# Linear attention and Fourier mixing on one core: an own front for the first batch, and a second fold of the channel transform

## The chip, the cores and the metric

The kernel runs on one core of a Trainium2 chip. The metric is the device time of one execution in microseconds. The kernel before takes 449.23 us (median of 3 runs, 448.87 to 451.64). Its profile is of one execution with a span of 447.7 us.

The core's engines are named as in the profile: PE (TensorE, with its weight loads as PEld), DVE (VectorE), ACT (ScalarE), POOL (GpSimd), and SP, whose queue issues stores and DMA transposes. Each engine takes its instructions in the order in which the program lists them.

## What is computed

There are 8 batches, 8 heads, 576 rows, a head size of 64 and 128 features. Per batch, attention with an exponential feature map gives a block of 576 x 512. Its two-dimensional Fourier transform (real part) is added to it, the sum is normalised by row, and two matrices with a ReLU between follow. Cut to the core:

```python
def phi(x):
    proj = einsum('bhsd,df->bhsf', x, w_phi)
    proj = proj - max(abs(proj), axis=-1, keepdims=True)
    return concatenate([exp(proj), exp(-proj)], axis=-1)

q_p, k_p = phi(q), phi(k)
kv = einsum('bhsf,bhsd->bhfd', k_p, v);  z = sum(k_p, axis=2)
x = (q_p @ kv) / (q_p @ z + 1e-6)            # heads side by side: 576 x 512
u = x + real(fft(fft(x, axis=rows), axis=channels))
un = (u - mean(u)) / sqrt(var(u) + 1e-6)     # per row
out = u + relu(un @ w_ch1) @ w_ch2           # 512 -> 2048 -> 512
```

Note that the second half of the features is exp(-proj + max), as the maximum is subtracted before the sign is turned.

## The kernel before

The program is one list of small steps. Each letter of `PLAN` takes the next step of one stream, and the order of the letters is the order of the instructions on every engine. The streams go through the batches one after the other, so steps of three batches stand side by side: `F` forward (68 steps a batch: hidden and output layer), `M` mixing (heads, Fourier transform), `D` row fold, `N` normalise, `T` the exponentials, `P` query maxima, `R` key maxima, `S` scaling of V, `K`, `V`, `Q` loads, `A`, `B` DMA transposes, `W` the large weights, `C` the tables of sines, `G`, `J` the turning of the first batch's K and Q on PE.

```python
PLAN = (
    "GCCGCTGJGCTJKQRJTRTSGTRPTSJTRTTSJMRMWTSSPTMTTBPMPTPVMTTMMMMMPTWATMPMMTMMMTTRRTDDSTMCRMSPTTMMTSTRMTTN"
    ...
```

The tables are made by C steps: DVE makes the angles, ACT takes the sines of them (SS, CS for the rows, SD, CD for the channels) before the first exponentials.

The exponentials of the queries in the feature step, both from one projection `psh`, without the maximum; the maximum of the negative half is put in later as the factor E2 = exp(2 max):

```python
psh = pj.tile([128, 2, 4, 128], F32, tag="pj", name="psh")
...
for sgn, QP in ((1.0, QPHP), (-1.0, QPHN)):
    nc.scalar.activation(out=o, in_=psh[:], func=AT.Exp, scale=sgn)     # L580
```

Numerator and denominator of a head, for all batches:

```python
def combine(h, kvh):
    pn_ = pj.tile([128, 2, 512], F32, tag="pj", name="pn_")
    for c in range(5):
        for i, QP in enumerate((QPHP, QPHN)):
            nc.tensor.matmul(pn_[:, i, 65 * c:65 * c + 65], lhsT=QP[:, h, ...], rhs=kvh[:, i, :],
                             start=True, stop=True)                      # L676
    nc.vector.tensor_tensor(out=tg[:], in0=Bv, in1=E2[...], op=ALU.mult)  # L683
    nc.vector.tensor_tensor(out=cb[:], in0=Av, in1=tg[:], op=ALU.add)     # L688
    nc.vector.reciprocal(out=rd[:], in_=cb[:, :, D:D + 1])                # L690
    nc.gpsimd.tensor_tensor(out=X[:, :, D * h:D * h + D], in0=cb[:, :, 0:D],
                            in1=rd[...], op=ALU.mult)                     # L691
```

The transform uses symmetry. Channels are folded once (FEO holds sums and differences of channel a and its mirror, L623), rows once (CEO and SE, L632 and L637). The first row of each fold is handled apart: it goes to a tile HI, a matmul with ones spreads it to all partitions, and it is subtracted:

```python
nc.scalar.copy(out=HI[0:1], in_=FEO[0:1, 0, :, :])                        # L645
...
pm = pb.tile([128, 2, 256], F32, tag="pb", name="pm")
nc.tensor.matmul(pm[:], lhsT=ones_b[:], rhs=HI[:], start=True, stop=True) # L716
nc.vector.tensor_tensor(out=CEO[0:64, 2], in0=FEO[0:64, 4], in1=pm[0:64], op=ALU.subtract)  # L717
nc.scalar.copy(out=CEO[64:65, 2, :, :], in_=pm[64:65])                    # L720
nc.vector.scalar_tensor_tensor(out=CEO[:, 0:2, 0, :], in0=pm[...], scalar=-2.0, in1=SE[:],
                               op0=ALU.mult, op1=ALU.add)                 # L721
```

The transform along the rows (psD, L737, twice 6 matmuls of 320 columns, and px, L745), then along the channels:

```python
for t in range(3):
    pu = pb.tile([128, C], F32, tag="pb", name="pu")
    for i, (dt_, mat) in enumerate(((DT, CD), (ET, SD))):
        for cc in range(2):
            nc.tensor.matmul(pu[:], lhsT=dt_[:, cc, 128 * t:128 * t + 128], rhs=mat[:, cc, :],
                             start=(i + cc == 0), stop=(i + cc == 2))     # L758
    ...                                                                   # added to X, L763 to L773
```

Normalising: statistics (L786, L787), UN = X - mean (L791 on ACT for the first batch, L795 on DVE for the others), and a DMA transpose to UT in all batches:

```python
nc.sync.dma_start_transpose(out=UT[:, :, 128 * c:128 * c + M], in_=UN[0:M, c, :])   # L799
```

The forward part: 2 halves of 288 rows, 16 x 4 matmuls each, a ReLU on ACT, then five row blocks of the output layer:

```python
for hf in range(2):
    for hh in range(NHH):
        ps = pb.tile([128, 288], F32, tag="pb", name="psf")
        for cc in range(NCC):
            nc.tensor.matmul(ps[:], lhsT=W1b[...], rhs=UT[:, cc, 288 * hf:288 * hf + 288], ...)  # L835
        nc.scalar.activation(out=HT[...], in_=ps[:], func=AT.Relu)        # L840
for c in range(4):
    for hh in range(NHH):
        nc.tensor.matmul(po[:], lhsT=HT[...], rhs=W2b[:, hh, :], ...)     # L847, 512 columns
    ...                                                                   # scaled, added, stored: L853
...                                                                       # last 64 rows: L862, L869
```

Of the kernel before, what the change touches and what calls it, by code (L numbers as in the profile page):

```python
# [17 lines left out]
MAGIC = 12582912.0  # L18


PLAN = (
    "GCCGCTGJGCTJKQRJTRTSGTRPTSJTRTTSJMRMWTSSPTMTTBPMPTPVMTTMMMMMPTWATMPMMTMMMTTRRTDDSTMCRMSPTTMMTSTRMTTN"
    "NRMMMTSMTTNPTMTPPPSMMPTMFFQPNFFMFTFKFFNMMFMFMFFFMFMFFMFMFFAFBFFFVPPTFRFFMFQTRFFFTPFFFFDFTPPRFFDFFTMN"
    "FTSFFSFFMFTFFMKRFSFMPTFFFRTSMMPFNTNNTTTFFFFFNMMSFFMFTTFMTFFTFFAFTFMNFFMNFFMFFMFFMFVPPFFFFMFMFFMFFBPT"
    "FMFFMFMFFMFRFFTPPFFFRFMTFFFFDTPFFRDFFFTFMFFFQTFFRMSTFFKFMMTRSFTFMFMSPFNNFNTTTFMMTFFFFSFFTTFTSFFMTFFF"
    "ATFMFFMNNFFFMNFFMFFVPPMFFMMFFMFFMFMFFFFBMFMFFPTRFFFTMFFFFRMSTFFFDFPPTFRFFDFFKFTFFMTFFFFRMFSFFTMMFTPF"
    "FRMQTSPFFMFSNNTTTNFFMNFMFFMFSFTMFFMTTFFTFFMTNFFMFFMTFNFFAMMFFMFFMFFFMFFFVPPBFFFTPFFMFFMFFMRFTFRFMFFT"
    "DFFFFPPTFFFFRFDFSFTMFKTSFFFMRFFFTMFMTPFFRMMNPFSFNTFNQTTTMMFFFFFMFSFTMFFMTTTFFFFMFTFMFSFFMNTFNFAMNFMF"
    "MFFFMFMFFBMFFPFMFFFVPPTFFFMFFFTRPPFFFRFMTFFDFKFTPFFFRDFSFFFTMFTFFRFSMFFTFMMTFFFRQMPFMTNFTNTSNTTFFFMM"
    "FSSFFFTTTFNFFMTAFFFTFMNFFMFFFMFFMFFNMFVPPFFFMMFMFFMFFMFFBMFFTPFMFFMFFFFRTMRFFTDFFDFFFFFPPTFMRFFFFFMS"  # L30
    "FTFSFSMFMPTFFRMTTNFFRPMNFNFTFFTFSNFFSTFTFFTFMMFTTFFFFTMTNFFMFFMFFMFFMFNFMTFFFMMMFFFMFFMFFMFMFFFFMFMF"
    "FFFFFFDFFFFDFFFFFMFFFFMMFMFFMNFNFFMFFNFFNFFFFFFFFFFFFMFNFFFFFFFFNFFFFFFFFFFFFFFFFFFFFFFFFFFFFFFFFFFF"
    "FFFFFFFFFFFFFFFFFFFFFFFF"
# [4 lines left out]
def kernel(  # L38
# [10 lines left out]
    nc = tc.nc  # L49
# [47 lines left out]
    CD = const.tile([128, 2, C], BF16, name="CD")  # L97
    SD = const.tile([128, 2, C], BF16, name="SD")


    HIS = [const.tile([128, 2, 256], BF16, name=f"HI{i}") for i in range(2)]
    CXS = [const.tile([128, 2, 128], BF16, name=f"CX{i}") for i in range(2)]
# [17 lines left out]
    pn = const.tile([128, 1], F32, name="pn")  # L120
    blk = const.tile([128, 3], F32, name="blk")
    tn = const.tile([128, 2, 128], F32, name="tn")
    ident = const.tile([128, 128], F32, name="ident")
    sg = const.tile([128, 2], BF16, name="sg")
# [7 lines left out]
    def count_all():  # L132
        count(tn[:, 0, :], [[1, 128]], 0, -1)
        for j in range(2):
            count(
                rs[:, 128 * j:128 * j + 128].rearrange("p (a r) -> p a r", r=16),
                [[-32, 8], [2, 16]], 225 + j, 0,
            )
        count(rs[:, 256:NK], [[1, 64]], 256, 0)
        nc.gpsimd.memset(rs[:, 256:257], 0.0)  # L140
        count(pc_i[:, 0:1], [[1, 1]], 0, 1)
        count(pc[:, 0:2], [[1, 2]], 225, 2)
        count(pc[:, 2:3], [[1, 1]], 256, 1)
        nc.gpsimd.memset(pc[0:1, 2:3], 0.0)
        nc.vector.tensor_single_scalar(
            out=ident[:], in_=tn[:, 0, :], scalar=0.0, op=ALU.is_equal
        )
        count(pc[:, 3:4], [[1, 1]], 0, 1)
        count(rc, [[1, C]], 0, 0)
        count(tn[:, 1, :], [[1, 128]], 0, 1)  # L150
        nc.gpsimd.memset(sg[:, 0:1], 1.0)
        nc.gpsimd.memset(sg[:, 1:2], -1.0)

    def constants(b):

        at, t0, t3 = gs[:, 0:3 * NK], gs[:, 1024:1024 + 3 * NK], ga[:, 0:3 * NK]
        scale = 2.0 * np.pi / S * (1.0 - 1e-7)
# [8 lines left out]
        nc.vector.tensor_tensor(  # L166
            out=at.rearrange("p (j n) -> p j n", n=NK),
            in0=rs.unsqueeze(1).to_broadcast([128, 3, NK]),
            in1=pc[:, 0:3].unsqueeze(2).to_broadcast([128, 3, NK]), op=ALU.mult,
        )  # L170
        nc.vector.tensor_scalar(
            out=t0, in0=at, scalar1=1.0 / S, scalar2=MAGIC, op0=ALU.mult, op1=ALU.add
        )
        nc.vector.tensor_scalar(
            out=t0, in0=t0, scalar1=MAGIC, scalar2=-float(S), op0=ALU.subtract, op1=ALU.mult
        )
        nc.vector.tensor_tensor(out=at, in0=at, in1=t0, op=ALU.add)
        nc.scalar.activation(
            out=SS[:].rearrange("p j n -> p (j n)"), in_=at, func=AT.Sin, scale=scale
        )  # L180
        nc.vector.scalar_tensor_tensor(
            out=t3, in0=at, scalar=-1.0, in1=at, op0=ALU.mult, op1=ALU.max
        )
        nc.scalar.activation(
            out=CS[:].rearrange("p j n -> p (j n)"), in_=t3, func=AT.Sin, scale=-scale,
            bias=halfpi[:],
        )
        yield

        t0 = gc[:, C:2 * C]  # L190
        tc2, tc3 = (gc[:, C * i:C * i + C] for i in (2, 3))
        scale_c = 2.0 * np.pi / C * (1.0 - 1e-7)
        nc.vector.tensor_scalar_mul(out=pn[:], in0=pc[:, 3:4], scalar1=1.0 / C)
        nc.vector.tensor_scalar(
            out=t0, in0=rc, scalar1=pn[:], scalar2=MAGIC, op0=ALU.mult, op1=ALU.add
        )
        nc.vector.tensor_scalar(
            out=t0, in0=t0, scalar1=MAGIC, scalar2=-float(C), op0=ALU.subtract, op1=ALU.mult
        )
        nc.vector.scalar_tensor_tensor(  # L200
            out=tc2, in0=rc, scalar=pc[:, 3:4], in1=t0, op0=ALU.mult, op1=ALU.add
        )
        nc.scalar.activation(out=SD[:, 0, :], in_=tc2, func=AT.Sin, scale=-scale_c)
        nc.vector.scalar_tensor_tensor(
            out=tc3, in0=tc2, scalar=-1.0, in1=tc2, op0=ALU.mult, op1=ALU.max
        )
        nc.scalar.activation(
            out=CD[:, 0, :], in_=tc3, func=AT.Sin, scale=-scale_c, bias=halfpi[:]
# [11 lines left out]
        yield  # L220
        for dst in (SS, CS):
            nc.gpsimd.memset(dst[64:65, 2, :], 0.0)
        nc.gpsimd.memset(CS[64:65, 2, 256:257], float(S))
        yield

        turn = sg[:].unsqueeze(1).to_broadcast([128, 128, 2])
        back = sg[:, ::-1].unsqueeze(1).to_broadcast([128, 128, 2])
        for dst, a, src, sign in (
            (CD, 0, CD, turn), (CD, 1, SD, turn), (SD, 0, SD, turn), (SD, 1, CD, back)
        ):  # L230
            nc.gpsimd.tensor_tensor(
                out=dst[:, 1, a::2].rearrange("p (n t) -> p n t", t=2),
                in0=src[:, 0, a::2].rearrange("p (n t) -> p n t", t=2),
                in1=sign, op=ALU.mult,
            )
        nc.gpsimd.memset(CD[0:1, 0, 0:C:2], 1.0)
        nc.gpsimd.memset(CD[0:1, 0, 1:C:2], 0.0)
        nc.gpsimd.memset(SD[0:1, 0, 0:C:2], 0.0)
        nc.gpsimd.memset(SD[0:1, 0, 1:C:2], 1.0)
        yield  # L240

    def clear_pads():
        nc.gpsimd.memset(QPHP[:, :, 576:640], 1.0)
# [58 lines left out]
    def load_first():  # L302
# [37 lines left out]
        for name in "KVQAB":  # L340
            taken[name] = 1
# [626 lines left out]
```

## Time and profile before

| what | measured |
|---|---|
| time, median of 3 runs | 449.23 us |
| span of the profiled execution | 447.7 us |
| mean granted clock of TensorE | 0.95 |
| weights W1b, W2b: issue to landing | 14.0 and 20.8 us |
| a load of K, Q, V: issue to landing | 5.4, 5.3, 6.8 us |
| DMA packets under 512 bytes | 85313 of 111088 |

The page of the profile gives, for each engine, its busy time and the share of the span. Below it the span is cut into 40 equal slices, 11.2 us each, with one digit per engine and slice: the busy share in tenths. The row PEclk is the clock granted to TensorE in tenths of full speed. A group of instructions is printed as line, engine, operation, output<-inputs, shape and count; behind the bar stand its busy time in us, the mean duration of one in ns, and the idle time of the engine just before them with what ended it. The first lines of the groups:

| group | count | mean of one, ns | sum, us |
|---|---|---|---|
| L835 PE, hidden layer, 288 columns | 1024 | 290 | 146.1 |
| L847 PE, output layer, 512 columns | 491 recorded | 379 | 121.4 |
| L840 ACT, ReLU | 256 | 413 | 102.9 |
| L623 POOL, channel fold | 59 | 864 | 49.8 |
| L485 DVE, key maxima | 32 | 1216 | 38.9 |

Durations of matmuls overlap, as matmuls are pipelined; the time from one start to the next tells more.

### The profile page before, as it was taken

Reading aid. Unit: us, or ns where it says so; the run is one execution under the profiler, and the core shown is the slowest. Engines: PE = TensorE matmul, PEld = TensorE weight load, DVE = VectorE, ACT = ScalarE, POOL = GpSimd, SP = SyncE. Lnnn points to the kernel's source line nnn. Section 1 sums busy time; section 2 is a strip of 40 time slices with the busy share of each in tenths; the row PEclk is TensorE's granted clock in tenths of the full one; section 3 lists DMA queues with packets and bytes.
Section 4 is the critical chain, followed back from the end, with each engine's and each line's share of the span. In section 5 each row is a group of like instructions: output and inputs, shape, how many; then the busy total and the mean of one; then the engine's idle time right before and its main releaser. Section 6 shows DMA issues by size and latency. Waiting matters only on the chain.

```text
span 447.7 us, 10078 instructions
## 1 busy us (share of the span) xinstructions
PE 402.4 (90%) x3937; PEld 254.9 (57%) x3964; DVE 324.1 (72%) x599; ACT 297.1 (66%) x617; POOL 268.2 (60%) x363
## 2 busy tenths in 40 slices
PE   3685378999979999899999999999879999999995
PEld 2454136864558546765587457744656548745742
DVE  8878866697938976697969787988658894758012
ACT  4994497777847788486777768777737688521810
POOL 7797847698437776589457964886538542911000
PEclk9976576999989999999999999999989999999999
DMA  8999919796692586807777596659890132015104
GB/s 218 213 160 170 204 27 99 98 117 61 131 171 49 48 118 130 132 1 87 115 134 92 59 139 123 93 70 124 134 115 2 23 67 73 3 17 112 31 8 99
DMA packets 111088, 43.27 MB, mean 97 GB/s; under 512 B 85313, under 2 KB 105921, under 8 KB 111041
## 3 DMA queue, kind: packets, MB, share of 16 engines
q0 software_dynamic: 45936, 16.60, 33.0%
q1 hardware_dynamic: 64945, 25.97, 31.7%
q8 instruction: 31, 0.51, 0.5%
q14 instruction: 16, 0.13, 0.1%
q10 hardware_dynamic: 160, 0.07, 0.1%
HBM read 36.77 MB, written 9.44 MB: 103 GB/s over the span
## 4 chain that ended last, share of the span: by engine, by line
PE 64%; DVE 15%; DMA 8%; ACT 6%; POOL 3%; issue 2%; SPq 1%; DVEq 0%; POOLq 0%
PE psf L835 24%; PE pso L847 18%; DMA QT<-QS 4%; PE pu L758 3%; DMA UT<-UN 3%; PE kv L661 3%; PE pso L862 3%; PE psD L737 2%; DMA out_dram<-X 2%; PE psh L571 2%; DVE MK L485 1%; PE psq L521 1%; PE psk L465 1%; DVE MQ L529 1%; DVE st L786 1%
## 5 line engine op out<-in xcount | busy, mean ns | idle before, releaser
L835 PE MATMUL psf<-UT,W1b 128*128 128x288 bf16 x1024 | 146.1, 290 | 3.5 <-DMA UT<-UN 3.4
L840 ACT ACTIVATE HT<-psf 128x288 bf16<-128x288 f32 x256 | 102.9, 413 | 59.3 <-PE psf L835 49.8
L847 PE MATMUL pso<-W2b,HT 128*128 128x512 bf16 x491 | 121.4, 379 | 1.3 <-issue 0.2
L835 PEld LDWEIGHTS <-W1b 128*128 128x128 bf16 x1024 | 94.5, 99 | 28.8 <-DMA UT<-UN 3.6
L691 POOL TENSOR_TENSOR X<-cb,rd 128x320 f32<-128x320 f32 x64 | 47.0, 738 | 55.0 <-DVE rd L690 55.0
L847 PEld LDWEIGHTS <-HT 128*128 128x128 bf16 x512 | 47.0, 98 | 52.0 <-issue 3.6
L529 DVE TENSOR_REDUCE MQ<-psq 128x8 f32<-128x1024 f32 (+1 forms) x40 | 39.3, 1005 | 18.7 <-PE psq L521 18.5
L623 POOL TENSOR_TENSOR FEO<-X 128x320 f32<-128x320 f32 x59 | 49.8, 864 | 2.2
L485 DVE TENSOR_REDUCE MK<-psk 128x8 f32<-128x1024 f32 x32 | 38.9, 1216 | 11.7 <-ACT KPp L471 6.9
L853 DVE SCALAR_TENSOR_TENSOR X<-pso,rs,X 128x512 f32<-128x512 f32 x32 | 23.7, 743 | 29.2 <-PE pso L847 29.2
L440 POOL TENSOR_TENSOR VCn<-VS,VCn 128x512 bf16<-128x512 bf16 x28 | 30.4, 1087 | 21.5 <-ACT VCn L435 21.1
L471 ACT ACTIVATE KPn<-psk 128x1024 bf16<-128x1024 f32 x32 | 32.7, 1022 | 11.9 <-DVE MK L485 11.7
L471 ACT ACTIVATE KPp<-psk 128x1024 bf16<-128x1024 f32 x32 | 32.7, 1022 | 7.1 <-PE psk L465 6.9
L580 ACT ACTIVATE QPHP<-psh 128x1024 bf16<-128x1024 f32 x32 | 33.2, 1037 | 5.7 <-PE psh L571 5.7
L809 POOL TENSOR_SCALAR VE<-MV 128x5 f32<-128x5 f32 x8 | 3.9, 488 | 49.1 <-DVE MV L787 49.0
L580 ACT ACTIVATE QPHN<-psh 128x1024 bf16<-128x1024 f32 x32 | 33.2, 1039 | 0.0
L440 POOL TENSOR_TENSOR VCp<-VS,VCp 128x512 bf16<-128x512 bf16 x28 | 30.3, 1080 | 0.0
L676 PEld LDWEIGHTS <-QPHP 128*128 128x128 bf16 x320 | 24.7, 101 | 5.2 <-DVE cb L688 3.4
L786 DVE BATCH_NORM_STATS2 st<-X 128x6 f32<-128x512 f32 (+1 forms) x40 | 27.3, 682 | 0.0
L795 DVE TENSOR_SCALAR UN<-X,MV 128x512 bf16<-128x512 f32 (+1 forms) x35 | 23.9, 683 | 1.4
L676 PEld LDWEIGHTS <-QPHN 128*128 128x128 bf16 x320 | 23.1, 99 | 2.0 <-issue 0.8
L669 ACT CAST kvh<-kv 128x130 bf16<-128x130 f32 x64 | 17.9, 286 | 8.6 <-PE kv L665 8.4
(408 smaller groups left out, 748.4 us busy)
## 6 DMA issues: line engine op xcount, KB each, us to landing
out_dram<-X SPq DMA_DIRECT2D x64, 64.0 KB
out_dram<-X SPq DMA_DIRECT2D x16, 256.0 KB
KS<-in_k_dram POOLq DMA_DIRECT2D x14, 256.0 KB, 5.4
QS<-in_q_dram POOLq DMA_DIRECT2D x14, 256.0 KB, 5.3
VS<-in_v_dram POOLq DMA_DIRECT2D x7, 512.0 KB, 6.8
W1b<-in_moe_w_ch_dram POOLq DMA_DIRECT2D x1, 2048.0 KB, 14.0
W2b<-in_moe_w_ch_dram POOLq DMA_DIRECT2D x1, 2048.0 KB, 20.8
W2b<-in_k_dram SPq DMA_DIRECT2D x2, 512.0 KB
```

Of the source, the lines that this page charges most:

```text
L440: nc.gpsimd.tensor_tensor(out=VC[:, hs, :, 0:D], in0=values[b][0][:, hs, :].rearrange("p h (j d) -> p h j d", d=D), in1=VC[:, hs, :, D:D + ...
L471: nc.scalar.activation(out=KP[:, hs, :, :].rearrange("p e (jp jj) f -> p jj (e jp) f", jj=2), in_=psk[:], func=AT.Exp, scale=sgn,)
L485: nc.vector.tensor_reduce(out=MK[:, 2 * pr:2 * pr + 2, :].rearrange("p e (jp jj) -> p jj (e jp)", jj=2), in_=tiles[pr][:], axis=AX.X, op=A ...
L529: nc.vector.tensor_reduce(out=o, in_=i[:], axis=AX.X, op=ALU.max, apply_absolute_value=True)
L580: nc.scalar.activation(out=o, in_=psh[:], func=AT.Exp, scale=sgn)
L623: eng.tensor_tensor(out=FEO[:, :, i, a:a + D], in0=X[:, :, a:a + D], in1=X[:, :, C - a:C - a - D:-1], op=op,)
L676: nc.tensor.matmul(pn_[:, i, 65 * c:65 * c + 65], lhsT=QP[:, h, 128 * c:128 * c + 128], rhs=kvh[:, i, :], start=True, stop=True,)
L691: nc.gpsimd.tensor_tensor(out=X[:, :, D * h:D * h + D], in0=cb[:, :, 0:D], in1=rd[:].to_broadcast([128, 5, D]), op=ALU.mult,)
L786: nc.vector.bn_stats(out=st[0:M, :], in_=X[0:M, c, 0:C])
L835: nc.tensor.matmul(ps[:], lhsT=W1b[:, cc, 128 * hh:128 * hh + 128], rhs=UT[:, cc, 288 * hf:288 * hf + 288], start=(cc == 0), stop=(cc == N ...
L840: nc.scalar.activation(out=HT[:, hh, 288 * hf:288 * hf + 288], in_=ps[:], func=AT.Relu)
L847: nc.tensor.matmul(po[:], lhsT=HT[:, hh, 128 * c:128 * c + 128], rhs=W2b[:, hh, :], start=(hh == 0), stop=(hh == NHH - 1),)
```

## The change

It has five parts.

1. **The channel transform is folded a second time, in all batches.** After the row step, channels k and 256 - k are added and subtracted (`again`), so that even and odd output channels each need 128 inputs where 256 stood. The row folds are written back into FEO in place; the tables CD and SD shrink from [128, 2, 512] to [128, 512]. The output comes out as even and odd channels apart and is added to X through a strided view.
2. **The first row is spread by a DMA** from SBUF to SBUF in batches 1 to 7, instead of by ACT, a matmul with ones and PSUM. In batch 0 the matmul stays.
3. **The first batch has an own front.** The exponential table is loaded at the start by a dummy activation, the sines come late (stream `H`). Negative query exponentials are made from a second projection into which a matmul adds -2 max (`pick`, the maxima turned into rows by `turn_m`), so that both halves add up in PSUM and a head needs one reciprocal and one product. Heads come in the order of pairs 0, 3, 2, 1, since head h folds with head 7 - h. The folds go to DVE, the statistics behind the forward start (`U`), the row sums for the mean come with the adds, and UN is turned by PE transposes.
4. **The forward order**: rows 0 to 255 hold blocks 0 and 2, so that the first hidden part needs two normalised blocks only. For batches 1 to 7 their output follows before the second hidden part (256 and 320 columns for 288 and 288).
5. **A new order of all steps.** K, V and Q loads are split into 3, 5 and 3 steps (V in 6 transfers where there were 3), and 16 steps of four matmuls whose result nobody reads (`Y`, `stir`) stand in the holes of the front. It is to start the first forward step sooner, and to take work from TensorE.

The diff, cut to its core:

```diff
-    CD = const.tile([128, 2, C], BF16, name="CD")
+    CD = const.tile([128, C], BF16, name="CD")
...
+    def sines(b):                       # stream H, placed late in the front
+        nc.scalar.activation(out=SS[...], in_=at, func=AT.Sin, scale=scale)
...
+        nc.scalar.activation(out=warm[:], in_=halfpi[:], func=AT.Exp)
...
+        def negative(t, outer):
+            ps = pj.tile([128, 2, 4, 128], F32, tag="pj", name="psn")
+            project(ps, t, outer, False)
...
+                    nc.tensor.matmul(
+                        ps[:, jj, x, :], lhsT=pick[:, k_:k_ + 1].to_broadcast([96, 128]), rhs=m,
+                        start=False, stop=(x == 3),
+                    )
+            result(t, outer, QPHN, ps, -1.0)
...
+        def combine(heads_, ps):        # batch 0
+            ...                         # both halves add up in PSUM
+            nc.vector.reciprocal(out=rd[:], in_=all_[:, :, :, D:D + 1])
+            nc.vector.tensor_tensor(out=X[...], in0=all_[:, :, :, 0:D], in1=rd[...], op=ALU.mult)
...
-            nc.scalar.copy(out=HI[0:1], in_=FEO[0:1, 0, :, :])
+            nc.sync.dma_start(
+                out=HI[:],
+                in_=FEO[0:1, 0, :, :].rearrange("p i n -> p (i n)").unsqueeze(1).to_broadcast(
+                    [1, 128, 512]
+                ),
+            )
...
+        def again(i):
+            for sgn, op in ((1, ALU.subtract), (0, ALU.add)):
+                j = sgn if i == 0 else 0
+                nc.vector.tensor_tensor(
+                    out=CEO[:, :, sgn, i, j:128], in0=FEO[:, 2:5, i, 128 - j:0:-1],
+                    in1=FEO[:, 2:5, i, 128 + j:256], op=op,
+                )
...
+        nc.vector.scalar_tensor_tensor(
+            out=flat[:, 2:4, 0:257], in0=pm[:, 0:257].unsqueeze(1).to_broadcast([128, 2, 257]),
+            scalar=-2.0, in1=flat[:, 2:4, 0:257], op0=ALU.mult, op1=ALU.add,
+        )
...
-            pu = pb.tile([128, C], F32, tag="pb", name="pu")
-            for i, (dt_, mat) in enumerate(((DT, CD), (ET, SD))):
-                for cc in range(2):
+            pu = pb.tile([128, 2, 256], F32, tag="pb", name="pu")
+            for n in range(2):
+                for i, (dt_, mat) in enumerate(((DT, CD), (ET, SD))):
                     nc.tensor.matmul(
-                        pu[:], lhsT=dt_[:, cc, 128 * t:128 * t + 128], rhs=mat[:, cc, :],
-                        start=(i + cc == 0), stop=(i + cc == 2),
+                        pu[:, n, :], lhsT=dt_[:, n, 128 * t:128 * t + 128],
+                        rhs=mat[:, 256 * n:256 * n + 256], start=(i == 0), stop=(i == 1),
                     )
...
+            if b == 0:
+                pt = pb.tile([128, NCC, M], BF16, tag="pb", name="put")
+                for cc in range(NCC):
+                    nc.tensor.transpose(pt[:, cc, :], UN[0:M, c, ...], ident_b[0:M, 0:M])
...
+            else:
+                nc.sync.dma_start_transpose(out=to, in_=UN[0:M, c, :])
...
+        for first, cs in ((True, slice(0, 3, 2)), (False, slice(0, 5))):   # rs of blocks 0, 2, then of all
+            nc.gpsimd.tensor_single_scalar(out=VE[:], in_=mv[:, cs, 1], scalar=1e-06, op=ALU.add)
+            nc.gpsimd.tensor_tensor(out=rs[:], in0=VE[:], in1=mhalf[:, 0:n], op=ALU.pow)
...
+        yield from hidden(0, 256)
+        if b == 0:
+            yield from hidden(256, S)
+        yield from output(0)
+        yield from output(2)
+        if b > 0:
+            yield from hidden(256, S)
+        yield from output(1)
+        yield from output(3)
...
+    def stir(b):
+        for i in range(16):
+            ps = pk.tile([128, 512], F32, tag="pk", name="idle")
+            for x in range(4):
+                nc.tensor.matmul(ps[:], lhsT=ones_b[:], rhs=ones_b[...], start=True, stop=True)
+            yield
```

## The prediction

> **What bounds the kernel now.** I read first the page's shares and slices, then busy time by stretch, cut at the first hidden-layer matmul (L835) of each batch, then the waits of TensorE, then the groups. The page:
>
> ```profile
> PE 402.4 (90%) x3937; PEld 254.9 (57%) x3964; DVE 324.1 (72%) x599; ACT 297.1 (66%) x617; POOL 268.2 (60%) x363
> ...
> PE   3685378999979999899999999999879999999995
> ...
> DVE  8878866697938976697969787988658894758012
> ...
> PEclk9976576999989999999999999999989999999999
> ```
>
> Each digit is 11.2 us. TensorE (PE) is full from the seventh slice on; before that it has holes, its granted clock falls to 0.5, and VectorE (DVE) is the fullest engine. So there are two regimes. By stretch (columns: window, length, busy us and instructions of PE, weight loads, DVE, ACT, POOL, then clock, DMA share, GB/s):
>
> ```profile
> 0.00:74.00 74.00, 45.32 (x476) 28.69 (x478) 59.73 (x114) 51.78 (x90) 56.36 (x94) 0.76 0.95 155
> 74.00:122.00 48.00, 47.43 (x475) 29.74 (x477) 38.23 (x72) 37.00 (x79) 34.65 (x45) 0.98 0.86 107
> ...
> 223.00:271.30 48.30, 48.09 (x508) 31.08 (x511) 38.48 (x69) 36.69 (x79) 32.94 (x42) 1.00 0.79 109
> ...
> 316.20:369.40 53.20, 48.48 (x478) 30.27 (x480) 39.09 (x71) 34.14 (x73) 28.27 (x35) 0.97 0.47 68
> ...
> 411.80:447.70 35.90, 30.42 (x198) 18.73 (x199) 5.84 (x9) 12.74 (x31) 1.72 (x2) 1.00 0.25 55
> ```
>
> The front is 74 us, with DVE busy 59.7, POOL 56.4 and ACT 51.8; no engine is full, so it is a chain across engines. Then batch follows batch, PE within 0.6 us of full, except where PE waits for data:
>
> ```profile
> PE psq L521 <- DMA QT<-QS: 5.4, 5, 1.6
> PE psf L835 <- DMA UT<-UN: 3.4, 2, 2.6
> ```
>
> (waits of PE from 74 to 444 us: total, times, longest). First L835 matmuls stand at 73.9, 121.8, 172.6, 223.0, 269.4, 316.0, 369.4 and 410.4 us. The front ends in a long transfer:
>
> ```profile
> 63.19 0.72 ACT L791 ACTIVATE UN<-X,nm 128x512 bf16<-128x512 f32 x1
> ...
> 63.93 14.40 SPq L799 DMA_TRANSPOSE UT<-UN  x4
> ```
>
> The first normalised rows exist at 63.9 us, the first L835 starts 10 us later.
>
> **What the Trainium skill says.** "TensorE: Matmul & The Clock Gate", section "Back-to-back issue gap": a warm stream advances by about N/2.4 + 2.5 ns per matmul of N columns, 216 ns for 512 and, by the same formula, 109 for 256 (an estimate; nothing of 256 full-array columns runs here). The trace agrees: the median from start to start is 216 ns at L847 and L758, though the page shows 379 and about 390 as duration. I therefore count starts, not durations. The same page, Part 1, says that an idle array falls to half clock; the trace has 0.50 granted from 40 to 56 us, where PE is 6.65 us busy of 16. "SBUF — State Buffer", section "Who interferes with whom": a DVE instruction with two SBUF inputs contends with a GpSimd one that reads SBUF. The trace fits:
>
> ```profile
> L637 DVE TENSOR_TENSOR SE<-FEO 128x384 f32<-128x384 f32 x7 | 7.3, 1041 | 0.0
> ...
> L177 DVE TENSOR_TENSOR gs<-gs 128x960 f32<-128x960 f32 x1 | 1.2, 1159 | 0.0
> ```
>
> 384 elements take 1041 ns in the crowded steady part, 960 take 1159 in the front, beside memsets. "ScalarE: Activation LUTs", section "What ACT_TABLE_LOAD costs": 1283 ns for a load; the trace has three, 1283 ns each.
>
> **Part 1, the second fold.** Per output tile the channel transform has 4 matmuls of 512 columns (L758), three tiles a batch: 12 x 216 = 2.59 us. Now it has 4 of 256: 12 x 109 = 1.31. Saved 1.28 us of PE. The row that was spread by a matmul (L716, one of 512 columns) is spread by DMA: 0.22 us more, batches 1 to 7. Together 1.5 us a batch; seven batches after the front, 10.5 us. PE's work per batch, from medians of start to start, is about 45.8 us (L835 128 x 0.122 = 15.6; L847 64 x 0.216 = 13.8; L862 1.85; L758 2.6; L737 and L745 2.05; L716 0.2; keyvalue and combine 160 x 0.032 = 5.1; projections and small ones 4.6). It becomes about 44.3.
>
> The price is on DVE. Four folds of 384 elements with two SBUF inputs are added: between 0.46 (the uncontended rate of 1.15 ns an element) and 1.04 us each, I choose 0.75, so 3.0. The -2 times subtraction reads SBUF where it read PSUM (0.69, now perhaps 1.0), the last block likewise (0.67, now 0.9), the small CX piece goes (0.16) and a copy comes (0.1). Sum: +3.5 us a batch, on 36.6 to 40.5 now, so about 41 to 42 of a 46 us period: 90%. ACT loses L645 and L720 (0.62 + 0.58 = 1.2 us). POOL gains a second pair of VE and rs (0.49 + 1.21 = 1.7) and three more V loads to issue (3 x 0.77 = 2.3): about 37 of 46. All of these lie beside matmuls of another batch; none is the bound, but DVE comes near.
>
> **Part 2, the front.** Gains on the chain to the first L835, each read in the trace: the three table loads and four sines stand in ACT between 7.5 and 14.3 us, and the first exponential starts at 14.28. With the table loaded ahead and the sines put late, it starts when the first keys are turned and projected, about 8.5: 6 us. From the last query exponentials (35 us) to the first UN (63.2) the old chain takes 28 us: eight combines with three DVE steps each (0.50 + 0.50 + 0.19 = 1.2 us a head) and a POOL product behind (0.72 to 0.97), folds on DVE and POOL at once (2.5 us for three), row fold, pm, psD, pu, statistics. The new one has the maxima inside the exponent, so a head needs a reciprocal and one product; only two pairs of heads remain after the last exponential. My sum: combine 2.0, fold 1.6, row fold 1.1, pm and last block 1.1, fold again 0.9, psD 1.5, second fold and psD 2.9, copies and px 1.3, pu 0.8, adds 1.55, UN 0.9, about 15.7 and 2.5 for handing over: 18 us, 10 less. The DMA transposes (10 us) become PE transposes and a copy: about 1.5, so 8 less. Against this: negative exponentials wait for the maxima, ACT makes more copies, and the fold runs on DVE: 6 back. 74 - 6 - 10 - 8 + 6 = 56 us for the first L835. The idle matmuls (64 of 512 columns) fill holes only; the clock near 1 that they buy is worth 1 to 2 us, in my margin.
>
> **Part 3, what the front hands on.** Much of these 18 us is work postponed. By the letters of the two step lists, ahead of the first forward step batch 1 had 17 of 18 feature steps (now 5), 6 of 7 query maxima (now 0), 5 of 5 key maxima (now 2) and 6 keyvalues (now 0). That puts 12 x 1.03 + 6 x 0.28 = 14 us on ACT and about 6 x 1.2 + 3 x 1.22 = 11 us on DVE into the next stretch, with 4.3 us of statistics of batch 0 (5 x 0.86) and part 1's 3.5: DVE 38.2 + 11 + 4.3 + 3.5 = 57, ACT 37 + 14 + 2 = 53, while PE has some 49. So DVE bounds this stretch, at about 58 us: the second batch's L835 starts at 56 + 58 = 114, against 121.8. Of 18 us, 8 stay.
>
> **Part 4, the six periods after.** They take 410.4 - 121.8 = 288.6 us, of which 6 x 45.8 = 275 is PE's work and 14 waits. New: 6 x 44.3 = 266 and waits. K, V and Q are fetched in more, smaller pieces and, by the list, more steps lie between turning Q and its first use (19 and now 31 in a batch I counted), so the QT and UT waits should mostly go; a DVE at 90% gives some back. I take 12: 278 us, to 392.
>
> **Part 5, the tail.** From the last batch's start to the end it is 447.7 - 410.4 = 37.3 us, nearly all lone matmuls of L835, L847 and L862. Their columns are unchanged (64 x 256 and 64 x 320 for 128 x 288). A little transform work slips in, so 37 to 38. The trace's end: 392 + 37.3 = 429.3, less rounding. Timed runs are 1.5 us above the span now (449.23 and 447.7). That would be near 431; as the front's sum is cautious, I choose 429.
>
> **Rivals.** (a) DVE takes over: if contention makes each added fold 1.04 us, DVE gains 4.7 and not 3.5, and combine and fold wait for it in strict order; periods stay at 47.5, and the time is 437 to 441. For it speaks the 1041 ns row; against it that PE has queued forward steps beside nearly every wait. (b) The front's gain is kept in full, because the postponed steps fit into idle ACT and DVE time of all later batches (some 20 and 25% idle now): 419 to 422. Against it: batch 1's features are needed within the first stretch. (c) The spreading DMA stands in the SP queue behind transposes and stores; if it lands 5 us late and the order leaves no cover, up to 7 x 2 us, 443. Speaks for it the QT wait above; against it, the next step on pm can be placed late. (d) The second fold is hidden anyway: only if PE weren't the bound, which the stretches contradict.
>
> **Range and chances.** The front is uncertain by 5 us either way, the first stretch by 4, six periods by 1 us each: about 8 together, rounded up to 11. So 418 to 440 holds it 8 times in 10. Two per cent is 440.2, at the edge of the range: faster 0.88, same 0.10, slower 0.02.
>
> **What would show it.** First L835 near 56 and the second batch's near 114 us; later starts 46 to 47 us apart; DVE at 41 us or more per period; pu matmuls starting 109 ns apart; UT waits gone in the first batch. Wrong would be: a front still past 65, a new PE wait on CEO or PM, DVE fold rows at a microsecond, or a first stretch over 65 us.

## The result, and the profile after

The changed kernel takes 500.8 us, the kernel before 449.8 us on the same chip (medians): a ratio of 1.113, with a 95% interval of 1.108 to 1.118. It is 51 us slower, where 20 us of gain were predicted. Cut where the prediction cut, at the first hidden-layer matmul of each batch (L835 in the kernel before, L1261 now), the spans divide as follows (us). The last three columns are experiments A, R and T, told below.

| | before | predicted | after | A | R | T |
|---|---|---|---|---|---|---|
| to the first batch's start | 73.9 | 56 | 61.0 | 56.5 | 60.2 | 60.1 |
| first stretch | 47.9 | 58 | 75.3 | 66.2 | 64.4 | 64.4 |
| six periods | 288.6 | 278 | 325.3 | 297.0 | 287.5 | 283.6 |
| tail | 37.3 | 37.3 | 38.8 | 39.1 | 39.0 | 39.4 |
| span | 447.7 | 429.3 | 500.4 | 458.8 | 451.1 | 447.5 |

The page of the changed kernel, first and second parts:

```profile
PE 427.3 (85%) x4103; PEld 264.9 (53%) x4103; DVE 339.9 (68%) x643; ACT 286.6 (57%) x613; POOL 282.7 (56%) x385
...
PE   7869799983999699967999569995999699949994
...
DVE  7968864883778567857886487874899388526402
...
PEclk9768999976899799997999797997999899978998
```

PE's row now has a hole at even distances, one in each batch: a 6, 5 or 4 between nines. DVE's row has a low digit at the same places, so it isn't busy there either. Both wait for a third. By stretch (window, length, busy us and instructions of PE, weight loads, DVE, ACT, POOL, then clock, DMA share, GB/s):

```profile
0.00:61.00 61.00, 47.96 (x477) 28.73 (x478) 48.72 (x104) 39.69 (x72) 36.41 (x64) 0.86 1.03 166
61.00:136.30 75.30, 63.11 (x611) 36.90 (x610) 49.89 (x96) 47.01 (x103) 50.96 (x66) 0.86 0.70 83
...
244.80:305.70 60.90, 50.47 (x489) 31.49 (x490) 43.94 (x73) 33.79 (x72) 40.60 (x54) 0.89 0.83 95
...
461.60:500.40 38.80, 32.10 (x214) 19.90 (x212) 10.56 (x18) 13.14 (x32) 1.72 (x2) 0.96 0.32 63
```

In the third of these lines PE is busy 50.5 us of 60.9, where it was 48.1 of 48.3 in a comparable stretch before. Its waits from 61 to 462 us (total, times, longest):

```profile
PE psD L1094 <- DVE CEO L1083: 41.0, 7, 7.6
PE pso L1297 <- DVE X L1139: 4.4, 1, 4.4
PE psf L1261 <- DMA UT<-UN: 2.9, 4, 1.0
```

The QT wait is gone and the UT wait is small, as meant. One new wait replaces them: the row transform psD waits for the fold (CEO) once in each of batches 1 to 7, and loses 41 us. The releaser is DVE, but DVE was itself waiting, by its own list of waits:

```profile
DVE FEO L1074 <- DMA PM<-FEO: 48.4, 7, 10.7
```

The timeline of one batch shows the links (start, length, engine, operation; in brackets the idle time before it and what ended it):

```profile
107.45 0.57 SPq L1012 DMA_DIRECT2D PM<-FEO  x1
...
118.87 0.75 DVE L1074 SCALAR_TENSOR_TENSOR FEO<-FEO,keep,PM 65x512 f32<-65x512 f32 x1 [7.63 <-DMA PM<-FEO]
119.65 1.03 DVE L1083 TENSOR_TENSOR CEO<-FEO 128x384 bf16<-128x384 f32 x2
...
120.27 1.78 PE L1094 MATMUL psD<-SS,CEO 128*128 128x320 bf16 x6 [7.61 <-DVE CEO L1083]
```

The transfer that spreads the row is issued at 107.45. The instruction that reads it starts 11.4 us later, and in strict order everything else on DVE, and then on PE, stands behind it. The page's list of transfers gives the landing time (KB each, median us from issue to landing):

```profile
PM<-FEO SPq DMA_DIRECT2D x7, 256.0 KB, 11.1
```

The trace dates the landing of one of the seven, the last; but in all seven batches DVE waits for the tile, and its reading instruction starts 11.2 to 11.5 us after the issue, in calm stretches as in crowded ones. So the transfer doesn't stand in a queue: it is itself that slow.

### The profile page after: what moved, and what is told of

Its sections match the earlier page's. It is cut to its first block, busy times and chain, and to the rows that moved or that the text cites. A ratio compares the mean times of both kernels' runs of the same rounds, so it can differ in the third digit from the quotient of the medians.

```text
span 500.4 us, 10436 instructions
## 1 busy us (share of the span) xinstructions
PE 427.3 (85%) x4103; PEld 264.9 (53%) x4103; DVE 339.9 (68%) x643; ACT 286.6 (57%) x613; POOL 282.7 (56%) x385
## 4 chain that ended last, share of the span: by engine, by line
PE 49%; DMA 19%; DVE 15%; POOL 12%; ACT 3%; issue 2%; POOLq 0%; DVEq 0%; SPq 0%; ACTq 0%
DMA PM<-FEO 16%; PE pso L1272 14%; PE psf L1261 13%; POOL FEO L1001 6%; PE psD L1094 4%; POOL X L1041 4%; PE kv L895 3%; DMA UT<-UN 2%; DVE UN L1194 2%; PE pso L1297 2%; PE idle L1350 2%; DVE CEO L1083 2%; DVE X L1139 2%; DVE cb L1038 1%; DVE FEO L1074 1%
## 5 line engine op out<-in xcount | busy, mean ns | idle before, releaser
L1261 PE MATMUL psf<-UT,W1b 128*128 128x320 bf16 (+1 forms) x1024 | 141.5, 286 | 4.5 <-DMA UT<-UN 2.9
L1272 PE MATMUL pso<-W2b,HT 128*128 128x512 bf16 x512 | 136.3, 400 | 0.0
L1265 ACT ACTIVATE HT<-psf 128x256 bf16<-128x256 f32 (+1 forms) x256 | 101.0, 422 | 46.9 <-PE psf L1261 38.4
L1261 PEld LDWEIGHTS <-W1b 128*128 128x128 bf16 x1024 | 95.2, 98 | 33.9 <-issue 5.2
L1272 PEld LDWEIGHTS <-HT 128*128 128x128 bf16 x512 | 47.4, 102 | 49.3 <-issue 11.8
L1094 PE MATMUL psD<-SS,CEO 128*128 128x320 bf16 (+1 forms) x48 | 13.5, 449 | 41.2 <-DVE CEO L1083 41.2
L1041 POOL TENSOR_TENSOR X<-cb,rd 128x320 f32<-128x320 f32 x56 | 39.9, 722 | 12.7 <-DVE rd L1040 11.1
L1231 POOL TENSOR_SCALAR VE<-MV 128x2 f32<-128x2 f32 (+1 forms) x16 | 6.3, 392 | 64.4 <-DVE MV L1219 63.7
L1094 PEld LDWEIGHTS <-CEO 128*128 128x128 bf16 (+1 forms) x96 | 11.0, 124 | 53.8 <-DVE CEO L1083 46.3
L1074 DVE SCALAR_TENSOR_TENSOR FEO<-FEO,keep,PM 65x512 f32<-65x512 f32 x7 | 5.2, 748 | 48.4 <-DMA PM<-FEO 48.4
L1139 DVE TENSOR_TENSOR X<-pu,X 128x512 f32<-128x512 f32 (+3 forms) x49 | 23.4, 529 | 11.1 <-PE pu L1149 11.1
L288 POOL DMA_DIRECT2D VS<-in_v_dram x42 | 30.1, 729 | 0.9 <-POOL VCp L474 0.6
## 6 DMA issues: line engine op xcount, KB each, us to landing
KS<-in_k_dram POOLq DMA_DIRECT2D x14, 256.0 KB, 11.8
PM<-FEO SPq DMA_DIRECT2D x7, 256.0 KB, 11.1
```

The lines of the kernel that those rows point to most:

```text
L288: nc.gpsimd.dma_start(out=pieces[i][0], in_=pieces[i][1])
L1094: nc.tensor.matmul(ps[:, mt, 0:NK], lhsT=CEO[0:R[c], c, abs(mt - i), i, :], rhs=mat[0:R[c], c, :], start=(c == 0), stop=(c == 2),)
L1139: nc.vector.tensor_tensor(out=to, in0=more, in1=to, op=ALU.add)
L1261: nc.tensor.matmul(ps[:], lhsT=W1b[:, cc, 128 * hh:128 * hh + 128], rhs=UT[:, cc, lo:hi], start=(cc == 0), stop=(cc == NCC - 1),)
L1265: nc.scalar.activation(out=HT[:, hh, lo:hi], in_=ps[:], func=AT.Relu)
L1272: nc.tensor.matmul(po[:], lhsT=HT[:, hh, at:at + 128], rhs=W2b[:, hh, :], start=(hh == 0), stop=(hh == NHH - 1),)
```

## The experiments

The theory to be tested: the slow transfer and the wait behind it make up the loss, and without it the change is worth what was predicted. The rivals: the transfer disturbs other transfers; the second fold costs more on VectorE than it saves on TensorE; TensorE's saved work buys nothing because other waits take its place; the new order brings waits of its own. The ratios, with 95% intervals, are to the kernel before on the same chip; times are medians, and both leave out the few runs in a slower state (one of A, three of S, some of the kernel before).

| run | what it is | us | ratio to before |
|---|---|---|---|
| A | the change, row spread by a matmul and a copy | 460.6 | 1.025 (1.019 to 1.032) |
| B | the change, the transfer with half the bytes | 483.4 | 1.075 (1.070 to 1.080) |
| C | A, and the same transfer into a tile nobody reads | 463.0 | 1.028 (1.023 to 1.034) |
| D | the kernel before, row spread by the transfer | 523.7 | 1.165 (1.158 to 1.172) |
| E | the kernel before, second fold alone | 459.2 | 1.018 (1.011 to 1.024) |
| F | A without the idle matmuls | 466.2 | 1.034 (1.026 to 1.041) |
| G | A, and a transfer of equal size read from 128 partitions | 463.5 | one run |
| H | A with the old order after the first stretch | 504.7 | 1.118 (1.110 to 1.126) |
| P | E with its channel-transform matmuls done twice | 461.2 | 1.021 (1.015 to 1.027) |
| R | A with the spread row kept in PSUM | 454.0 | 1.005 (1.003 to 1.008) |
| S | the kernel before, half of the channel transform left out | 450.3 | 0.997 (0.994 to 1.000) |
| T | R with one tile normalised by ScalarE | 449.4 | 0.998 (0.996 to 1.000) |

### A, B, C: is it the wait?

A puts the matmul back in all batches and keeps front, fold and order:

```diff
-            nc.sync.dma_start(out=HI[:], in_=FEO[0:1, 0, :, :]....to_broadcast([1, 128, 512]))
+            nc.scalar.copy(out=(HI0, HI1)[b % 2][0:1], in_=FEO[0:1, 0, :, :])
...
-            pm = HI
+            nc.tensor.matmul(ps_[:], lhsT=ones_b[:], rhs=(HI0, HI1)[b % 2][...], start=True, stop=True)
+            nc.scalar.copy(out=HI[:], in_=ps_[:])
+            pm = HI
```

> The changed kernel, but the first row is spread in batches 1 to 7 too by ACT copy, a matmul with ones and an ACT copy to PM; the order of steps is kept. Theory T (the transfer itself: all 128 packets read one partition, it lands after 11.1 us, and the wait for it stops VectorE and then TensorE): the gaps of TensorE before the first psD matmul of batches 1 to 7 (7.8, 4.8, 6.6, 5.7, 5.5, 4.9, 6.9 us, 42 in all) go, and some clock comes back: about 453 us. Rival O (the new order and the added folds on VectorE are what costs): it stays above 480 us.

It takes 460.6 us: 40.2 of the 51 us are gone. The wait itself falls from 41.0 us to this (from the first to the last batch's start):

```profile
PE psD L1097 <- DVE CEO L1086: 5.8, 5, 1.7
```

That the 40.2 us are so near the 41.0 of the wait is partly chance. Between the first and the last batch's start, all waits of PE together fall by 26.4 us only (52.9 to 26.5), as other waits grow, and its busy time falls by 10.9 us (347.2 to 336.3), with a granted clock of 0.97 where the changed kernel had 0.91. The rest of the change, however, is still 2.5% slower than the kernel before. The first theory holds for the loss and fails for the gain.

B keeps the transfer with the row in bf16, so 128 KB:

```diff
-        HI = fpool.tile([128, 512], F32, tag="PM", name="PM")
+        HI = fpool.tile([128, 512], BF16, tag="PM", name="PM")
+        HR = fpool.tile([1, 512], BF16, tag="HR", name="HR")   # the row, copied by ScalarE, is what is spread
```

> The changed kernel with the row first made bf16 by ACT, so that the DMA moves 128 packets of 1 KB where it moved 2 KB. T says that the transfer goes with the bytes read from the one partition: landing 11.1 -> about 6.7 us, each of the 7 waits 4.4 us shorter, 470 us. Rival Q (the DMA waits in the SP queue behind stores and transposes, or a fixed cost): landing stays near 11 us and the time near 500 us.

The tile's own answer in the trace of B:

```profile
DMA to landing us min/median/max: 6.3/6.3/6.3
```

Half the bytes take 4.8 us less to land, and the kernel 17.4 us less, about half of 7 x 4.8 and less than expected. The copy by ScalarE that B adds accounts for the rest. First PE's wait in all, then three lines of one batch:

```profile
PE psD L1093 <- DVE CEO L1082: 25.6, 6, 5.6
...
157.15 0.62 ACT L1013 CAST HR<-FEO 1x512 bf16<-1x512 f32 x1
157.79 0.56 SPq L1014 DMA_DIRECT2D PM<-HR  x1
164.36 0.75 DVE L1073 SCALAR_TENSOR_TENSOR FEO<-FEO,keep,PM 65x512 f32<-65x512 f32 x1 [6.41 <-DMA PM<-HR]
```

In this batch GpSimd's last fold of the row ends at 151.9, but the copy stands behind other work of ScalarE, so the transfer is issued 5.9 us later. In four of the seven batches this lag is 4.2 to 5.9 us; in the changed kernel it is 0.03 us in six of seven.

C does A's matmul and sends the same 256 KB into a tile that nobody reads:

```diff
+            nc.scalar.copy(out=(HI0, HI1)[b % 2][0:1], in_=FEO[0:1, 0, :, :])
             nc.sync.dma_start(
-                out=HI[:],
+                out=PX[:],
```

> As a_mm, but the DMA of the changed kernel still runs, into a tile that nobody reads. T (only the wait costs): within 3 us of a_mm. Rival L (the 9 us in which all DMA engines read one partition hold up loads, transposes and stores of the others): 10 us or more above a_mm.

C is 2.4 us above A by the medians, 1.2 by the ratios, and the runs of the two overlap, although its transfer lands as late. The loads beside it do feel it; the second of these lines is from C, the third from A:

```profile
PX<-FEO SPq DMA_DIRECT2D x7, 256.0 KB, 11.1
KS<-in_k_dram POOLq DMA_DIRECT2D x14, 256.0 KB, 11.3
KS<-in_k_dram POOLq DMA_DIRECT2D x14, 256.0 KB, 5.0
```

So the transfer more than doubles the landing time of the K loads that are issued next to it, and the changed kernel shows the same (11.8 us). But C's trace shows no engine waiting for these loads: in time, the transfer costs hardly more than the wait for its own tile.

### G: why is the transfer slow?

```diff
-            nc.sync.dma_start(out=PX[:], in_=FEO[0:1, 0, :, :]....to_broadcast([1, 128, 512]))
+            nc.sync.dma_start(out=PX[:], in_=FEO[:, 0, :, :].rearrange("p i n -> p (i n)"))
```

> The row is spread by a matmul, and beside it a transfer of the same 256 KB, in 128 packets of 2048 B on the same queue, goes from all 128 partitions of the tile (no spreading) into a tile that nobody reads. Theory one partition (the slowness comes from all packets being read from one partition): it lands after 2 to 4 us. Rival queue (a transfer of this size and form at this place is slow whatever it reads): it lands after 9 us or more. The time says little here; about 460 to 465 us by both.

```profile
PX<-FEO SPq DMA_DIRECT2D x7, 256.0 KB, 4.0
```

Queue, size, place and target are those of C; only the source differs, 128 partitions instead of one. 11.1 us become 4.0 (in both traces the landing is dated for the transfer of the last batch), so it is the source that makes it slow. From B and after, 128 KB cost 4.8 us, which is 27.3 GB/s, with about 1.5 us left over that doesn't go with the bytes. The Trainium skill bears on this, though the prediction doesn't use it: "SBUF — State Buffer", section "Door 1: The DMA port swizzle (why [64,N] ≈ [32,N])", gives about 27 GB/s for a transfer that reaches only partitions 0 to 3, one port of sixteen. By that figure 262144 bytes take an estimated 9.7 us before any fixed part, and the trace agrees: 11.1 less 1.5 is 9.6. A spread row reaches 128 partitions on its writing side and one on its reading side, and here the narrower side sets the rate. G differs from C in a second point, as it reads every byte once where the spread reads one row 128 times; the runs don't part the two, and only the agreement with the page's figure speaks for the partition.

### D: the same transfer in the old order

```diff
-            nc.scalar.copy(out=HI[0:1], in_=FEO[0:1, 0, :, :])
+            nc.sync.dma_start(out=PM[:]..., in_=FEO[0:1, 0, :, :]....to_broadcast([1, 128, 512]))   # batches 1 to 7
```

> The kernel before with one thing of the change: the row is spread by the DMA in batches 1 to 7. T: the same wait in the old order, 5 to 8 us in each of 7 batches: 485 to 505 us. Rival O: under 460 us.

It is 73 us slower, more than any of the expectations had. The waits of PE from 74 to 482 us:

```profile
PE psD L749 <- DVE CEO L729: 59.3, 7, 9.4
PE psq L521 <- DMA QT<-QS: 5.9, 4, 2.2
```

59.3 us of the 73 are that wait, 8.5 us a batch against 5.9 in the changed kernel: the new order does cover a part of the landing. The rest lies in PE's own work: from the first to the last batch's start PE is busy 342.6 us where it was 325.5 in the kernel before, with a granted clock of 0.91 instead of 0.99. (D also keeps one tile HI instead of two and lets a table of the front share memory with another; its first batch starts at 73.9 us as before.)

### E, P and S: what is the second fold worth?

A left a loss of some 11 us. E brings the second fold alone into the kernel before, with its front, its order and its spread by matmul:

```diff
+        again(1)
         nc.vector.scalar_tensor_tensor(out=flat[:, 2:4, 0:257], in0=pm..., scalar=-2.0, in1=flat[:, 2:4, 0:257], ...)
+        again(0)
...
-            pu = pb.tile([128, C], ...)        # 4 matmuls of 512 columns a tile
+            pu = pb.tile([128, 2, 256], ...)   # 4 matmuls of 256
```

> The kernel before with the second fold of the channel transform alone; the row is spread by the matmul into PSUM as before, front and order of the steps are those of before. Theory S (the fold takes 1.3 us of TensorE from each of 8 batches and its price on VectorE lies beside other work): about 440 us. Rival V (the longer chain on VectorE from pm to psD stops TensorE in each batch): 450 to 456 us.

459.2 us: the fold, meant to save, costs 9 us, more than the rival's 450 to 456. The waits of PE from 74 to 444 us show a line that the kernel before doesn't have:

```profile
PE psD L737 <- DVE CEO L743: 4.9, 6, 1.4
PE psf L836 <- DMA UT<-UN: 4.2, 4, 1.4
PE psD L737 <- DVE CEO L719: 3.0, 5, 1.0
```

PE waits 7.9 us for the folded tiles: the DVE instructions between pm and psD are longer, and nothing lies in between. The first batch also starts at 76.3 us instead of 73.9. To part price and saving, P pays the price without the saving (every matmul of 256 columns is done twice, the first sum overwritten), and S takes the saving without the price (half of the matmuls into `pu`, and so half of the sum, are left out):

```diff
 P  -            for n in range(2):
    +            for n in (0, 0, 1, 1):
 S  -                for cc in range(2):
    +                for cc in range(1):
```

> The second fold alone, with each of its channel-transform matmuls done twice (the first sum is overwritten): the price on VectorE without the saving on TensorE, 24 x 109 ns as in the kernel before. Theory sum (saving and price are each paid in full): about 459 + 9 = 468 us. Rival chain (VectorE's longer chain sets the time, TensorE's saved time was idle anyway): 458 to 461 us.

> The kernel before with half of the matmuls of the channel transform left out (two of four per output tile, so half of the sum is missing; every other operation is there): the saving of Part 1 without its price. Theory work (TensorE's work sets the periods): 12 x 216 ns - 6 x 216 ns = 1.3 us a batch, seven to eight batches, 9 to 10 us: 440 to 442 us. Rival waits (the saving falls into waits of the fixed order): 446 to 450 us.

Both theories miss, and both times lie at the upper edge of what the rivals said. P is only 2.0 us slower than E (less than the spread of either), and S only 1.1 us faster than the kernel before on the same chip: in this order, 1.3 us of TensorE work a batch, 9 to 10 us in all, are worth 1 to 2. The waits of PE from 74 to 444 us in S say why:

```profile
PE psf L835 <- DMA UT<-UN: 7.1, 4, 4.2
PE psq L521 <- DMA QT<-QS: 4.3, 4, 1.7
PE pso L862 <- DVE X L773: 1.7, 1, 1.7
PE psf L835 <- DVE X L869: 1.1, 3, 0.5
```

Before, the UT wait was 3.4 us and no wait on X appeared. All PE waits of that window together were 9.5 us before and are 16.6 us in S: 7.1 us of the saving came back as waits for transposes and for VectorE's sums. TensorE was full, but only just the fullest: in the old order the chain over VectorE and the transposes is as long, and becomes the limit as soon as TensorE gets shorter.

### F: the idle matmuls

```diff
-            for x in range(4):
-                nc.tensor.matmul(ps[:], lhsT=ones_b[:], rhs=ones_b..., start=True, stop=True)   # 512 columns each
```

> a_mm without the 64 idle matmuls of stream Y. If they only fill holes: within 3 us of a_mm. If the clock that they keep up is worth something (a_mm's front ran at 0.94): 4 us or more slower. If they stand in the way of the chain (the trace of the changed kernel has them on the chain from 44 to 50 us): 3 us or more faster.

Without them A is 4 us slower by the ratios and 6 by the medians (466.2). The front by stretch:

```profile
0.00:63.90 63.90, 38.73 (x416) 26.42 (x417) 48.13 (x104) 40.03 (x72) 37.08 (x65) 0.73 1.00 167
```

PE has 61 instructions less, the granted clock is 0.73 instead of 0.94 in A, and the first batch starts at 63.9 instead of 56.5 us. A's profile is the best of its kind: with the idle matmuls the other profiles of this front have clocks of 0.86 to 0.91 and starts of 59.3 to 61.6 us. The intervals of F and A overlap, so the size is uncertain; the clock and the start point the same way.

### H: the old order with the new steps

H keeps A's steps and puts the rest of `PLAN`, from the second batch's start on, into the order of the kernel before.

> a_mm with the new order up to the first hidden matmul of batch 1 and from there the old order of the steps, in the new steps' granularity. Theory P (beyond the DMA, the new order of the steady part costs: its six periods take 297 us where the old ones took 288.6 with more matmul work): periods as of before less 1.5 us each, 280 us in all, 441 to 446 us. Rival: the old order does no better with the new steps, 458 us or more.

It takes 504.7 us, far over the theory's 441 to 446; the rival had "458 us or more". The waits of PE from 60 to 462 us:

```profile
PE psq L557 <- DMA QT<-QS: 26.8, 8, 8.5
PE psD L1097 <- DVE CEO L1086: 10.7, 7, 3.0
```

The new steps fetch K, Q and V in more pieces. Packed where the old order had one step each, the turned queries come up to 8.5 us late. The run therefore says that order and pieces belong together, and it doesn't isolate the order.

### R and T: what else stood in A

A's own row goes through a copy by ScalarE into SBUF, and in one batch VectorE's folds took 1.4 us each and the subtraction 3.07 instead of 0.69, beside GpSimd's products. R keeps the row in PSUM and does both subtractions in one step, in batches 1 to 7:

```diff
-            nc.scalar.copy(out=HI[:], in_=ps_[:])
-            pm = HI
+            pm = ps_          # keep and the -2 times subtraction follow at once, for b > 0
```

> The changed kernel with the row spread by a matmul as in the first experiment, but the spread row stays in PSUM: the copy by ScalarE goes, both subtractions read PSUM and stand in one step, in batches 1 to 7. Theory contention and hand-over (the copy and the second SBUF input cost): 3.5 us at most for the wait on the copy and some 6 us in the one crowded batch go in part, 454 to 459 us. Rival order (other waits of the new order take their place): 460 to 464 us.

454.0 us, 7 less than A by the medians and 9 by the ratios. PE's wait for psD falls from 5.8 to 0.4 us, and where VectorE waited 13.8 us for ScalarE's copy, it waits 6.1 us for the matmul. R changes three things at once (no copy, PSUM as the source, the second subtraction earlier), and no run parts them. One larger gap of PE is left, in the period from 222 to 276 us (A and the changed kernel have it too, with 4.4 us), and what goes with it is on the timeline of VectorE and GpSimd in R:

```profile
PE pso L1305 <- DVE X L1147: 4.3, 1, 4.3
```

```profile
263.24 0.78 DVE L1202 TENSOR_SCALAR UN<-X,MV 128x512 bf16<-128x512 f32 x1
...
264.87 5.42 DVE L1202 TENSOR_SCALAR UN<-X,MV 128x512 bf16<-128x512 f32 x1
264.90 1.05 POOL L476 TENSOR_TENSOR VCp<-VS,VCp 128x512 bf16<-128x512 bf16 x1
265.92 1.05 POOL L476 TENSOR_TENSOR VCn<-VS,VCn 128x512 bf16<-128x512 bf16 x1
...
268.96 1.05 POOL L476 TENSOR_TENSOR VCp<-VS,VCp 128x512 bf16<-128x512 bf16 x1
270.21 1.93 DVE L1147 TENSOR_TENSOR X<-pu,X 128x512 f32<-128x512 f32 x4
```

The same instruction takes 0.49 us as a median of all 35 and 5.42 here. Five products of GpSimd (VCp and VCn, 1.05 us each) run without a pause from 264.90 to 270.01. "SBUF — State Buffer", section "Who interferes with whom", counts the DVE operation with a scalar operand among those that can take both ports, and says that then one of the two engines is shut out and not merely slowed. The trace fits this, and shows more than one such turn: the instruction ends 0.3 us after the last of the five products. That the products are what holds it up rests on this coincidence; no run takes them away. T gives this one tile to ScalarE:

```diff
+                if b == 4 and c == 2:
+                    nc.vector.tensor_scalar_mul(out=nm[0:M, :], in0=mv[0:M, c, 0:1], scalar1=-1.0)
+                    nc.scalar.activation(out=UN[0:M, c, :], in_=X[0:M, c, 0:C], func=AT.Identity, bias=nm[0:M, :])
```

> The version with the spread row in PSUM (454.0 us), and one normalisation of one tile (third block of the fifth batch) done by ScalarE in place of VectorE. There VectorE's 128x512 instruction, elsewhere 0.49 us, took 5.42 us while GpSimd ran five products of 1.05 us in a row, and TensorE stood still for 4.35 us behind VectorE. Theory port (VectorE is kept out by GpSimd's row of products only in an instruction that reads and writes SBUF alone): the wait of 4.35 us goes, 449.5 to 451 us. Rival (the next VectorE instruction is kept out in its place, or ScalarE's extra 0.6 us delays the matmuls): 453 to 455 us.

```profile
265.04 0.15 DVE L1204 TENSOR_SCALAR nm<-MV 128x1 f32<-128x1 f32 x1
265.11 1.93 DVE L1147 TENSOR_TENSOR X<-pu,X 128x512 f32<-128x512 f32 x4
```

VectorE's additions, which read PSUM and SBUF, now start 5 us earlier and take the same 1.93 us; the period falls from 54.0 to 49.9 us and the time to 449.4 us, 4.6 less than R by the medians and 3.2 by the ratios. That is the change without its transfer, its copy and this one hold-up, and it equals the kernel before: the interval of the ratio, 0.996 to 1.000, leaves room for no more than 0.4%.

## Why the prediction was wrong, step by step

**The transfer (rival c), mis-sized.** The mechanism was named: a late landing without cover stops the chain. The size was taken as "5 us late" and "up to 7 x 2 us", and the cause as the queue. No transfer of this size in the kernel before reads one partition only, so the trace held no row for it. It lands after 11.1 us and costs 40.2 us (A), not 14. The argument against it, that "the next step on pm can be placed late", doesn't hold for the new list: the first reader of PM is the next mixing step, and the strict order puts everything else behind it.

**Part 1 and Part 4, the premise that failed.** "Saved 1.28 us of PE" is right in columns: matmuls into `pu` start 109 ns apart, as estimated. (The section "Back-to-back issue gap", cited there, gives its formula for a matmul alone and a shorter spacing for a stream, 131 ns at 512 columns; the trace of the kernel before has 216 ns in its streams, and that decides.) That a saved us of PE is a saved us of time was wrong. It was read from PE being "within 0.6 us of full". S leaves the work out and gains 1 us of the 9 to 10. Part 1's price was right in size (an added fold takes 0.55 us without contention, not 0.75; 384 elements at the 1.15 ns named there would be 0.44, not 0.46), but it was called "beside matmuls of another batch"; in the old order it lies between pm and psD, where it costs 7.9 us of PE waits (E). In the new order that wait is 5.8 us in A and 0.4 us in R. Rival (d), that the fold is "hidden anyway", was dismissed because the stretches seemed to contradict it; S and P show it to be the nearest to the truth for the old order. In the new order, with the obstacles gone, the six periods take 283.6 us (T): 5.0 less than before, where 10.6 were predicted. How much of this is the fold's and how much the order's, no run parts. Rival (a), a VectorE that takes over, is right for the chain, not for its busy time: DVE is busy 38 to 45 us in each of the five periods of A that are 48 to 56 us long.

**Part 2, the front: right in kind.** 56 us was predicted. Profiles of the same front have 56.5 (A), 59.3 (B), 60.2 (R), 61.0 (after) and 61.6 (C), with granted clocks from 0.94 down to 0.86: the agreement of A is luck, and about 60 the usual. The idle matmuls seem to be worth more than the "1 to 2 us" assumed (F).

**Part 3, what the front hands on: the wrong engine.** It was to be 58 us, bound by DVE at 57, with "PE some 49". The first stretch of A:

```profile
56.50:122.70 66.20, 59.69 (x612) 35.66 (x611) 49.75 (x96) 47.57 (x105) 51.24 (x66) 0.95 0.74 94
```

DVE is busy 49.8 us, PE 59.7, with 612 instructions instead of some 475. The step list that gave 12 feature steps and 6 keyvalues to ACT and DVE gave their matmuls to PE too, and these were left out of the sum: psq has 80 matmuls here where it had 40, psh 16 for 8, psk 48 for 32, kv 110 for 60. The stretch is 66 us long, and the second batch starts at 122.7 us in A against 121.8 before. Of 17.4 us gained in front nothing is left. That PE's added work sets this length is read from the line above; no run takes that work out.

**What is left without the transfer.** Had the row spread been hidden, the prediction would still have missed. T's span is 18.2 us over the predicted one: 4.1 us in front, 6.4 in the first stretch, 5.6 in the six periods, 2.1 in the tail.

**Part 5, the tail:** 38.8 us instead of 37 to 38, a small miss; its cause stays open.

**What would show it wrong** was listed correctly: "a new PE wait on CEO or PM" and "a first stretch over 65 us" are both there. The chances were not in keeping with that list.

## What to carry to other kernels

Before a row is spread by a transfer, look at the narrower side: one source partition gave 27 GB/s here, and a matmul with ones did the same work inside the stream. An engine that is 99% busy in a stretch is not proof that its work sets the time; leave some of that work out and run it, for if a second chain is as long, hardly anything moves. When work is postponed out of a stretch, add it to every engine that its steps use, the fullest one first.

## What the runs showed of the hardware that was not expected

- 256 KB spread from one partition land after 11.1 us, 128 KB after 6.3, and 256 KB from 128 partitions after 4.0 (after, B, G; one dated landing each). Loads of 256 KB beside the first kind land after 11.3 us instead of 5.0 (C against A).
- A DVE instruction of 0.49 us that reads and writes SBUF took 5.42 us beside five GpSimd products in a row, and one such event moved a kernel of 450 us by 3 to 5 us (R and T).
- The front's granted clock was 0.73 without the sixty idle matmuls (F) and 0.86 to 0.94 with them (eight profiles); the time was 4 to 6 us shorter with them, in intervals that overlap (A and F).
